# Keys split in halves over partition groups, a product with v over 64 rows in four tiles, and four raw pieces of w_out in flight

## The chip, the cores and the metric

One core of a Trainium2 chip. The metric is the time of one execution on the device in microseconds (us), as the median of several executions. The trace of one execution of each kernel was read as well; its span is about 2 us below the time of the same execution.

A ratio is the mean time of one kernel's runs over that of the kernel before in the same rounds, with a 95% interval. It is not quite the ratio of the medians quoted beside it.

## The reference, cut to what matters

```python
scores = scale * np.matmul(q, k.transpose(0, 1, 3, 2))          # (8, 8, 576, 576)
thresh = np.max(scores, axis=-1, keepdims=True) - tau
scores = np.where(scores >= thresh, scores, -1000000000.0)
attn = np.exp(scores - np.max(scores, axis=-1, keepdims=True))
attn = attn / (np.sum(attn, axis=-1, keepdims=True) + 1e-09)
out  = np.matmul(attn, v)                                       # head_dim 64
# x = out as (4608 tokens, 512)
g = x @ w_gate;  silu = g * (1.0 / (1.0 + np.exp(-g)))          # 512 -> 1536
y = (silu * (x @ w_val)) @ w_out                                # 1536 -> 512
```

Each softmax row needs one maximum and one sum over all 576 keys. That is what the change cuts in two.

## The kernel before: the parts that matter

The kernel walks over segments (a pair of heads of one batch element) and in each over tiles of 128 queries, five to a full segment. The last has 64 queries. While VectorE and ScalarE do the softmax of a tile, TensorE gets a portion of the feed-forward network (gate, value and output products, called fill here). The scores of a tile take both buffers of the PSUM pool `ps_s`. The product with v of the *previous* segment comes during the first tile of a segment and takes its outputs from the same pool.

```python
ps_s = ctx.enter_context(tc.tile_pool(name="ps_s", bufs=2, space=bass.MemoryType.PSUM))
...
def scores(seg, t):
    pss = [ps_s.tile([P, 2, 512], F32, name="sc") for _ in range(2)]       # both buffers
    ... # 4 matmuls: 128 queries x 288 keys, for two heads
    for h in range(m):
        nc.vector.tensor_reduce(out=nmx[:, h:h + 1], in_=scs[h], axis=AX.XY, op=ALU.max, negate=True)
    for h in range(m):
        nc.scalar.activation(ps[h], scs[h], AF.Exp, bias=nmx[:, h:h + 1])
    nc.scalar.activation(th[:, 0:m], nmx[:, 0:m], AF.Identity, bias=cut, scale=-1.0)
    yield
    turn()                                            # transposes of the tile before
    for h in range(m):                                # masking and sum: frees the score buffers
        nc.vector.scalar_tensor_tensor(out=ps[h], in0=scs[h], scalar=th[:, h:h + 1], in1=ps[h],
                                       op0=ALU.is_ge, op1=ALU.mult, accum_out=sm[:, h:h + 1])
    ... # + 1e-9, reciprocal; yield; scaling on ScalarE
...
for n, seg in enumerate(segs):
    for x, t in enumerate(seg["tiles"]):
        go = scores(seg, t); next(go)                 # scores, maxima, exponentials
        ...
        next(go); ...; fill(part); next(go)           # masking, a portion of fill, scaling
        if attends and not alone:                     # first tile of a segment
            next(products); next(products)            # product with v, copies out
        ...
        fill(part)                                    # the other portion
```

## Time and profile before

| | kernel before |
|---|---|
| time | 1779.55 us (1779.41 to 1782.08, 3 runs) |
| first 30 tiles (attention alone, then weights arriving) | 329.3 us |
| the long stage: the other 130 tiles, from their first scores to the last | 1225.8 us |
| from there to the end | 211.5 us |
| TensorE in the long stage: idle, at half clock | 50.8 us, 0 us |

The stages are cut at the start of a tile's scores in the trace, so that the same work lies in each stage of every kernel; the 9 to 10 us before the first scores are left out. The views are in the prediction below.

### The profile page before, as it was taken

What the parts mean: (1) busy time and instruction counts of PE and PEld (TensorE: products, weight loads), DVE (VectorE), ACT (ScalarE), POOL (GpSimd) and SP (SyncE); (2) the same over time, 40 slices, a digit from 0 to 9 for tenths busy, and PEclk for the clock granted to TensorE, in tenths of its full rate; (3) what the DMA queues carried; (4) which work ended last, traced back from release to release, by engine and by line L of the source; (5) the groups of instructions that cost most, each with busy time, mean ns of one, the idle gap of its engine ahead of it and who ended that gap; (6) DMA issues with size and microseconds to landing.
All of it is one profiled execution on the core that took longest, in us unless ns stands there. A gap on an engine that the chain in (4) does not pass through costs nothing.

```text
span 1776.2 us, 35271 instructions
## 1 busy us (share of the span) xinstructions
PE 1587.2 (89%) x15008; PEld 917.8 (52%) x15008; DVE 897.4 (51%) x1978; ACT 708.4 (40%) x1274; POOL 302.1 (17%) x246
## 2 busy tenths in 40 slices
PE   4577862799999999999999999999999999999998
PEld 3444430366855545545555555545545555555554
DVE  7876675465555545555545444544554544521000
ACT  4554542245443535434434443534434434411111
POOL 3233334201110201111010110211011101101111
PEclk9678885799999999999999999999999999999999
DMA  6545122222212121221122122121122112100000
GB/s 165 134 119 140 40 73 71 67 59 48 41 41 53 38 61 35 48 53 20 41 47 51 30 47 53 41 59 31 25 46 54 36 40 52 28 19 1 6 12 18
DMA packets 179179, 90.75 MB, mean 51 GB/s; under 512 B 157520, under 2 KB 163664, under 8 KB 179024
## 3 DMA queue, kind: packets, MB, share of 16 engines
q1 hardware_dynamic: 176144, 79.07, 19.6%
q0 software_dynamic: 2880, 9.44, 1.4%
q8 instruction: 118, 1.93, 0.5%
q14 instruction: 37, 0.30, 0.1%
HBM read 79.04 MB, written 9.44 MB: 50 GB/s over the span
## 4 chain that ended last, share of the span: by engine, by line
PE 75%; issue 5%; DVE 2%; DMA 1%; ACT 1%; POOL 1%; SPq 0%; POOLq 0%; DVEq 0%; ACTq 0%
PE po L356 19%; PE pg L323 19%; PE pv L331 19%; PE xo L273 9%; PE sc L206 7%; PE sc L213 2%; DMA ht<-in_moe_w_out_dram 1%; DVE tmp L149 0%; DVE p L228 0%; POOL tmp L155 0%; DVE tmp L151 0%; POOL ht L342 0%; ACT gt L341 0%; DVE nmx L221 0%; DVE p L244 0%
## 5 line engine op out<-in xcount | busy, mean ns | idle before, releaser
L356 PE MATMUL po<-wo,ht 128*128 128x512 f32 x864 | 397.4, 611 | 52.9 <-POOL wo L158 52.0
L323 PE MATMUL pg<-xT,wg 128*128 128x384 f32 (+1 forms) x1248 | 411.1, 473 | 11.2 <-POOL wg L158 9.1
L331 PE MATMUL pv<-xT,wv 128*128 128x384 f32 (+1 forms) x1248 | 409.3, 472 | 0.4 <-ACT xT L301 0.4
L221 DVE TENSOR_REDUCE nmx<-sc 128x1 f32<-128x576 f32 x288 | 205.6, 750 | 312.9 <-PE sc L206 289.0
L223 ACT ACTIVATE p<-sc,nmx 128x576 f32<-128x576 f32 x288 | 203.4, 741 | 304.8 <-DVE nmx L221 304.2
L323 PEld LDWEIGHTS pg<-xT,wg 128*128 128x128 f32 x1248 | 231.0, 193 | 162.5 <-issue 23.6
L331 PEld LDWEIGHTS pv<-xT,wv 128*128 128x128 f32 x1248 | 230.3, 192 | 152.1 <-issue 25.6
L234 ACT ACTIVATE p<-p,ri 128x576 f32<-128x576 f32 x288 | 209.2, 768 | 218.4 <-DVE ri L231 218.3
L356 PEld LDWEIGHTS po<-wo,ht 128*128 128x128 f32 x864 | 162.3, 193 | 258.3 <-issue 198.1
L228 DVE SCALAR_TENSOR_TENSOR p<-sc,th,p 128x576 f32<-128x576 f32 x288 | 220.5, 797 | 32.3 <-ACT th L224 32.3
L332 DVE TENSOR_TENSOR ht<-gt,pv 128x384 f32<-128x384 f32 (+1 forms) x156 | 80.2, 517 | 283.3 <-PE pv L331 258.8
L273 PE MATMUL xo<-p,vr 32*64 32x128 f32 (+2 forms) x8352 | 170.3, 292 | 53.1 <-issue 42.9
L244 DVE STREAM_TRANSPOSE p<-p 128x576 f32<-128x576 f32 x288 | 207.1, 753 | 0.9 <-ACT p L234 0.9
L342 POOL TENSOR_TENSOR ht<-ht,gt 128x768 f32<-128x768 f32 (+1 forms) x78 | 130.0, 1695 | 444.1 <-ACT gt L341 384.2
L273 PEld LDWEIGHTS xo<-p,vr 32*64 32x64 f32 x8352 | 146.7, 131 | 87.6 <-issue 67.1
L324 ACT COPY gt<-pg 128x384 f32<-128x384 f32 (+1 forms) x156 | 70.1, 449 | 240.3 <-PE pg L323 240.3
L206 PE MATMUL sc<-kT,qT 64*128 64x288 f32 x896 | 143.1, 433 | 5.1 <-DVE p L228 5.1
L186 POOL TENSOR_SCALAR qraw<-qraw,scl 128x576 f32<-128x576 f32 x32 | 55.6, 1737 | 437.1 <-DMA qraw<-in_q_dram 366.3
L206 PEld LDWEIGHTS sc<-kT,qT 64*128 64x128 f32 x896 | 79.0, 188 | 85.7 <-issue 71.2
L293 DVE COPY xT<-xo 128x128 f32<-128x128 f32 (+2 forms) x57 | 13.9, 285 | 175.7 <-PE xo L273 175.7
L361 POOL DMA_DIRECT2D out_dram<-ob x36 | 20.7, 574 | 420.4 <-ACT ob L360 420.4
L360 ACT COPY ob<-po 128x512 f32<-128x512 f32 x36 | 21.0, 584 | 119.0 <-PE po L356 79.7
(51 smaller groups left out, 747.3 us busy)
## 6 DMA issues: line engine op xcount, KB each, us to landing
vr<-in_v_dram SPq DMA_DIRECT2D x280, 144.0 KB, 3.4
qraw<-in_q_dram SPq DMA_DIRECT2D x128, 72.0 KB, 2.3
kraw<-in_k_dram SPq DMA_DIRECT2D x128, 72.0 KB, 2.7
out_dram<-ob POOLq DMA_DIRECT2D x36, 256.0 KB, 2.3
wo<-in_moe_w_gate_dram SPq DMA_DIRECT2D x16, 384.0 KB, 4.3
wo<-in_moe_w_val_dram SPq DMA_DIRECT2D x16, 384.0 KB, 4.4
ht<-in_moe_w_out_dram SPq DMA_DIRECT2D x16, 384.0 KB, 3.0
tau_s<-in_tau_dram SPq DMA_DIRECT2D x1, 0.5 KB
```

The lines of the kernel that those rows point to most:

```text
L206: nc.tensor.matmul(pss[h][:, n, 0:SH], qT[hs, q0:q0 + P], kT[hs, n * SH:(n + 1) * SH], start=True, stop=True)
L221: nc.vector.tensor_reduce(out=nmx[:, h:h + 1], in_=scs[h], axis=AX.XY, op=ALU.max, negate=True)
L223: nc.scalar.activation(ps[h], scs[h], AF.Exp, bias=nmx[:, h:h + 1])
L228: nc.vector.scalar_tensor_tensor(out=ps[h], in0=scs[h], scalar=th[:, h:h + 1], in1=ps[h], op0=ALU.is_ge, op1=ALU.mult, accum_out=sm[:, h:h ...
L234: nc.scalar.activation(ps[h], ps[h], AF.Copy, scale=ri[:, h:h + 1])
L244: nc.vector.transpose(out=p, in_=p)
L273: nc.tensor.matmul(xa[a][h * D:(h + 1) * D, at:at + n * G].rearrange("d (t r) -> d t r", r=G), vr[rs, h, j, :], p[rs, lo:hi, js], start=(j ...
L323: nc.tensor.matmul(ps[:, 0:n], wg[:, c, f * P:(f + 1) * P], x[:, c, cs], start=(c == 0), stop=(c == NCC - 1))
L331: nc.tensor.matmul(ps[:, 0:n], wv[:, c, f * P:(f + 1) * P], x[:, c, cs], start=(c == 0), stop=(c == NCC - 1))
L332: nc.vector.tensor_tensor(out=hts[f // 2][:, f % 2, cs], in0=gts[f // 2][:, f % 2, cs], in1=ps[:, 0:n], op=ALU.mult)
L342: nc.gpsimd.tensor_tensor(out=ht, in0=ht, in1=gt, op=ALU.mult)
L356: nc.tensor.matmul(po, hts[f // 2][:, f % 2, i * P:(i + 1) * P], wo[:, f, :], start=(f == 0), stop=(f == NF - 1))
```

## The change

Its intent: a product with v that contracts over 64 keys in place of 32. That is 72 records on four 64*64 tiles (18 rounds) in place of 288 on eight 32*64 tiles (36 rounds, 7.10 us in the mean of the late products). For this, two groups of 32 partitions must hold two different halves of the keys for the *same* queries. The scores are laid out so from the start: partition group (a, c) holds query group a and key half c. The price is that a row's maximum and sum lie in two groups and must be exchanged (`across`). Besides, v is loaded into two buffers, and w_out arrives in four raw buffers instead of two, with two conversions to a tile.

The diff, cut to its core:

```diff
-                            land2[len(wpieces) % 2]))
+                            land2[len(wpieces) % 4]))
 ...
+    def across(x, n):
+        y = stp.tile([P, 4], F32, name="other")
+        for g in range(NG):
+            nc.vector.tensor_copy(y[g * G:(g + 1) * G, 0:n], x[(g ^ 1) * G:((g ^ 1) + 1) * G, 0:n])
+        return y[:, 0:n]
 ...  # scores: 16 matmuls of 32 output partitions and 288 columns in place of 4 of 128
-        for h in range(m):
-            nc.vector.tensor_reduce(out=nmx[:, h:h + 1], in_=scs[h], axis=AX.XY, op=ALU.max, negate=True)
-        for h in range(m):
-            nc.scalar.activation(ps[h], scs[h], AF.Exp, bias=nmx[:, h:h + 1])
+        for x, tile_ in enumerate(pss):
+            nc.vector.tensor_reduce(out=nmx[:, 2 * x:2 * x + 2], in_=tile_[:, :, 0:SH], axis=AX.X, op=ALU.max,
+                                    negate=True)
+        nc.vector.tensor_tensor(out=nmx[:, 0:m], in0=nmx[:, 0:m], in1=across(nmx, m), op=ALU.min)
+        for x in range(m):                                   # m is 4 now, 2 before
+            nc.scalar.activation(ps[x], scs[x], AF.Exp, bias=nmx[:, x:x + 1])
 ...
-        nc.vector.tensor_scalar(out=sm[:, 0:m], in0=sm[:, 0:m], scalar1=1e-9, scalar2=None, op0=ALU.add)
+        nc.vector.scalar_tensor_tensor(out=sm[:, 0:m], in0=sm[:, 0:m], scalar=1e-9, in1=across(sm, m),
+                                       op0=ALU.add, op1=ALU.add)
 ...  # product with v
-            xo = [ps_s.tile([P, 2, 512], F32, name="xo", tag="sc") for _ in range(2)]
-        for j in range(NJ):
-            for a in range(NG):
-                rs = slice(a * G, (a + 1) * G)
+            xo = ps_s.tile([P, 2, 512], F32, name="xo", tag="sc")
+        for j in range(NK):                                  # NK = NJ // 2
+            for a in range(2):
+                rs = slice(a * D, (a + 1) * D)
 ...  # pacing of the conversions
-            if alone and n >= NP:
+            if n >= NP:
                 weights(1)
```

More of the change, by code (lines that the diff above doesn't have):

```diff
@@ L54 @@
     NJ = S // G
+    NK = NJ // 2
     SM = 512
@@ L113 @@
     land2 = [hp.tile([P, 2, TC], F32, name="ht").rearrange("p n w -> p (n w)") for _ in range(2)]
+    spare = xp.tile([P, NCC, TC // (2 * G), 2, G], F32, name="xT").rearrange("p c t a r -> p (c t a r)")
+    land2 += [spare[:, n * 2 * TC:(n + 1) * 2 * TC] for n in range(2)]
     for f in range(0, NF, nf):
@@ L123, in fetch_weights @@
         for _ in range(n):
-            if not wpieces or len(fetched) + len(split) >= (NL if len(wpieces[0][0].shape) == 2 else 2):
+            if not wpieces or len(fetched) + len(split) >= (NL if len(wpieces[0][0].shape) == 2 else 4):
                 return
@@ L190, in load_v @@
         b, hp_ = divmod(i, NP)
-        vr = ld.tile([P, 2, NJ, D], F32, name="vr")
-        for a in range(NG):
-            for h in range(2):
-                nc.sync.dma_start(out=vr[a * G:(a + 1) * G, h],
-                                  in_=v[b, 2 * hp_ + h].rearrange("(r j) d -> r j d", r=G))
-        return vr
+        vr = ld.tile([P, 2, NK, D], F32, name="vr", bufs=2)
+        for a in range(2):
+            for c in range(2):
+                nc.sync.dma_start(out=vr[(2 * a + c) * G:(2 * a + c + 1) * G].rearrange("r h j d -> r h (j d)"),
+                                  in_=v[b, 2 * hp_:2 * hp_ + 2].rearrange("h (r c j) d -> c r h (j d)", c=2, j=NK)[c])
+        return vr
+    def across(x, n):
[3 more added lines that the diff above has]
+        return y[:, 0:n]
     def scores(seg, t):
@@ L203, in scores @@
             pss = [ps_s.tile([P, 2, 512], F32, name="sc") for _ in range(2)]
-            for n in range(2):
-                for h, hs in enumerate(heads):
-                    nc.tensor.matmul(pss[h][:, n, 0:SH], qT[hs, q0:q0 + P],
-                                     kT[hs, n * SH:(n + 1) * SH], start=True, stop=True)
+            put = [(pss[h], u, h, q0 + u * D) for u in range(2) for h in range(2)]
             at = [tiles.index(t), len(tiles) + tiles.index(t)]
@@ L210, in scores @@
             pss = [ps_s.tile([P, 2, 512], F32, name="sc")]
-            for n, h in ((0, 0), (1, 1), (1, 0), (0, 1)):
-                hs = heads[h]
-                nc.tensor.matmul(pss[0][hs, n, 0:SH], qT[hs, q0:q0 + 2 * G], kT[hs, n * SH:(n + 1) * SH],
-                                 start=True, stop=True)
+            put = [(pss[0], h, h, q0) for h in range(2)]
             at = [tiles.index(t)]
-        m = len(at)
-        nmx, th, sm, ri = (stp.tile([P, 2], F32, name=x) for x in ("nmx", "th", "sm", "ri"))
-        scs = [ps[:, :, 0:SH] for ps in pss]
-        ps = [pt[:, x, :].rearrange("p (n s) -> p n s", n=2) for x in at]
-        for h in range(m):
-            nc.vector.tensor_reduce(out=nmx[:, h:h + 1], in_=scs[h], axis=AX.XY, op=ALU.max, negate=True)
-        for h in range(m):
-            nc.scalar.activation(ps[h], scs[h], AF.Exp, bias=nmx[:, h:h + 1])
+        for x in range(0, len(put), 2):
+            for g in range(NG):
+                a, c = divmod(g, 2)
+                for ps, u, h, col in put[x:x + 2]:
+                    hs = heads[h]
+                    nc.tensor.matmul(ps[g * G:(g + 1) * G, u, 0:SH], qT[hs, col + a * G:col + (a + 1) * G],
+                                     kT[hs, c * SH:(c + 1) * SH], start=True, stop=True)
+        m = 2 * len(at)
+        nmx, th, sm, ri = (stp.tile([P, 4], F32, name=x) for x in ("nmx", "th", "sm", "ri"))
+        scs = [ps[:, u, 0:SH] for ps in pss for u in range(2)]
+        ps = [pt[:, x, u * SH:(u + 1) * SH] for x in at for u in range(2)]
+        for x, tile_ in enumerate(pss):
[4 more added lines that the diff above has]
+            nc.scalar.activation(ps[x], scs[x], AF.Exp, bias=nmx[:, x:x + 1])
         nc.scalar.activation(th[:, 0:m], nmx[:, 0:m], AF.Identity, bias=cut, scale=-1.0)
@@ L226, in scores @@
         turn()
-        for h in range(m):
-            nc.vector.scalar_tensor_tensor(out=ps[h], in0=scs[h], scalar=th[:, h:h + 1], in1=ps[h],
-                                           op0=ALU.is_ge, op1=ALU.mult, accum_out=sm[:, h:h + 1])
-        nc.vector.tensor_scalar(out=sm[:, 0:m], in0=sm[:, 0:m], scalar1=1e-9, scalar2=None, op0=ALU.add)
+        for x in range(m):
+            nc.vector.scalar_tensor_tensor(out=ps[x], in0=scs[x], scalar=th[:, x:x + 1], in1=ps[x],
+                                           op0=ALU.is_ge, op1=ALU.mult, accum_out=sm[:, x:x + 1])
+        nc.vector.scalar_tensor_tensor(out=sm[:, 0:m], in0=sm[:, 0:m], scalar=1e-9, in1=across(sm, m),
+                                       op0=ALU.add, op1=ALU.add)
         nc.vector.reciprocal(out=ri[:, 0:m], in_=sm[:, 0:m])
         yield
-        for h in range(m):
-            nc.scalar.activation(ps[h], ps[h], AF.Copy, scale=ri[:, h:h + 1])
+        for x in range(m):
+            nc.scalar.activation(ps[x], ps[x], AF.Copy, scale=ri[:, x:x + 1])
         for x in at:
@@ L252, in attend @@
         full = [t for t in tiles if t < NT]
-        m = len(full)
+        m = 2 * len(full)
+        p = p.rearrange("p n (u j q) -> p (n u) j q", u=2, q=G)
         if alone:
-            xa = [ps_f.tile([P, 512], F32, name="xa", tag="psf") for _ in range(NG)]
+            xa = [ps_f.tile([P, 512], F32, name="xa", tag="psf") for _ in range(2)]
         else:
-            xo = [ps_s.tile([P, 2, 512], F32, name="xo", tag="sc") for _ in range(2)]
-            xa = [xo[a // 2][:, a % 2, :] for a in range(NG)]
-        for j in range(NJ):
-            js = slice(j * G, (j + 1) * G)
-            for a in range(NG):
-                rs = slice(a * G, (a + 1) * G)
-                for h in range(2):
-                    lo = len(tiles) if h else 0
-                    hi = lo + m
-                    at = P
-                    if tail and h == 0 and a < 2:
-                        hi += 1
-                    if tail and h == 1 and a >= 2:
-                        lo -= 1
-                        at -= G
-                    n = hi - lo
+            xo = ps_s.tile([P, 2, 512], F32, name="xo", tag="sc")
+            xa = [xo[:, a, :] for a in range(2)]
+        for j in range(NK):
+            for a in range(2):
+                rs = slice(a * D, (a + 1) * D)
+                for h in range(2):
+                    lo = h * (m + tail)
+                    at = G - h * tail * G
+                    n = m + tail
                     nc.tensor.matmul(
-                        xa[a][h * D:(h + 1) * D, at:at + n * G].rearrange("d (t r) -> d t r", r=G),
-                        vr[rs, h, j, :], p[rs, lo:hi, js], start=(j == 0), stop=(j == NJ - 1))
+                        xa[a][h * D:(h + 1) * D, at:at + n * G].rearrange("d (i q) -> d i q", q=G),
+                        vr[rs, h, j, :], p[rs, lo:lo + n, j, :], start=(j == 0), stop=(j == NK - 1))
         yield
@@ L280, in attend @@
         per = TC // (2 * G)
-        for w in range(2):
-            put = nc.scalar.copy if w or alone else nc.vector.tensor_copy
-            ts = [first + 2 * t + w for t in full]
-            for j in sorted({x // per for x in ts}):
-                own = [x for x in ts if x // per == j]
-                t0 = ts.index(own[0])
-                dst = xts[j][:, cc, own[0] % per:own[-1] % per + 1:2].rearrange("d t a r -> d a t r")
-                cs = slice(P + t0 * G, P + (t0 + len(own)) * G)
-                if alone:
-                    for a in range(2):
-                        put(dst[:, a], xa[2 * w + a][:, cs].rearrange("d (t r) -> d t r", r=G))
-                else:
-                    put(dst, xo[w][:, :, cs].rearrange("d a (t r) -> d a t r", r=G))
+        puts = deque([nc.scalar.copy] if alone else [nc.vector.tensor_copy, nc.scalar.copy])
+        blocks = [first + 2 * t + u for t in full for u in range(2)]
+        for j in sorted({x // per for x in blocks}):
+            own = [x for x in blocks if x // per == j]
+            i0 = 1 + blocks.index(own[0])
+            dst = xts[j][:, cc, own[0] % per:own[-1] % per + 1]
+            cs = slice(i0 * G, (i0 + len(own)) * G)
+            if alone:
+                for a in range(2):
+                    puts[0](dst[:, :, a, :], xa[a][:, cs].rearrange("d (i q) -> d i q", q=G))
+            else:
+                puts[0](dst.rearrange("d i a q -> d a i q"), xo[:, :, cs].rearrange("d a (i q) -> d a i q", q=G))
+            puts.rotate(1)
         if tail:
@@ L297, in attend @@
                 hs = slice(h * D, (h + 1) * D)
-                c0 = P + m * G if h == 0 else P - G
+                cs = slice((1 + m) * G, (2 + m) * G) if h == 0 else slice(0, G)
                 if alone:
                     for a in range(2):
-                        nc.scalar.copy(xts[j][hs, cc, at, a], xa[2 * h + a][hs, c0:c0 + G])
+                        puts[0](xts[j][hs, cc, at, a], xa[a][hs, cs])
                 else:
-                    (nc.scalar.copy if h else nc.vector.tensor_copy)(xts[j][hs, cc, at], xo[h][hs, :, c0:c0 + G])
+                    puts[0](xts[j][hs, cc, at], xo[hs, :, cs])
+                puts.rotate(1)
         yield
@@ L530 @@
             if not alone:
-                if wpieces or fetched or split:
-                    weights(1)
+                weights(1)
             elif n >= NP or n * len(early) + x < 2 * NCC:
```

## The prediction

> **What bounds the kernel now.** I read the page first (busy shares, slices), then the waits of TensorE by stage, then single stretches of the timeline.
>
> ```profile
> PE 1587.2 (89%) x15008; PEld 917.8 (52%) x15008; DVE 897.4 (51%) x1978; ACT 708.4 (40%) x1274; POOL 302.1 (17%) x246
> PE   4577862799999999999999999999999999999998
> DVE  7876675465555545555545444544554544521000
> ```
>
> Each digit is a slice of 44.4 us. There are three stages: attention alone to 177 us, in which VectorE (DVE) is fuller than TensorE (PE); a stretch to 333 us with a hole in PE; then PE at nine tenths or more. The same by stage (columns PE, PEld, DVE, ACT, POOL, clock, DMA):
>
> ```profile
> 177.00:258.00 81.00, 64.91 (x744) 38.12 (x744) 53.83 (x118) 36.95 (x68) 27.09 (x24) 0.85 0.23 54
> 258.00:333.00 75.00, 23.00 (x40) 8.40 (x40) 43.45 (x76) 22.50 (x40) 33.80 (x31) 0.59 0.26 75
> 333.00:1570.00 1237.00, 1186.24 (x11132) 687.62 (x11128) 650.20 (x1452) 534.03 (x928) 157.03 (x114) 1.00 0.19 44
> ```
>
> The middle row is PE waiting for pieces of w_out. PE's waits before 330 us, and the chain of waits there:
>
> ```profile
> PE po L356 <- POOL wo L158: 52.0, 4, 19.0
> PE sc L206 <- DVE p L228: 35.0, 10, 4.5
> ...
> 296.68 3.06 DMA ht<-in_moe_w_out_dram
> 304.04 3.02 DMA ht<-in_moe_w_out_dram
> 311.35 3.05 DMA ht<-in_moe_w_out_dram
> ```
>
> A load of 3 us stands in the chain every 7.35 us, and each such turn makes two pieces: two raw buffers, so 3.67 us a piece. After 333 us PE is the bound, and what can be won there is PE time. One product with v there, on the PE timeline:
>
> ```profile
> 560.94 0.49 PE L273 MATMUL xo<-p,vr 32*64 32x160 f32 x8 [0.59 <-PE pg L323]
> 561.68 4.04 PE L273 MATMUL xo<-p,vr 32*64 32x128 f32 x220 [0.24 <-issue]
> 566.61 1.33 PE L273 MATMUL xo<-p,vr 32*64 32x160 f32 x60 [0.89 <-issue]
> 567.87 2.85 PE L331 MATMUL pv<-xT,wv 128*128 128x384 f32 x8
> ```
>
> From 560.94 to 567.87 is 6.93 us for 288 records. In the single records each of the eight 32*64 tiles starts a 160-column record every 136 ns, so 36 rounds should take 4.9 us. The rest is a halt after eight records (they await the second head's masking on VectorE) and the 0.89 us halt at "issue". Such halts stand 128 records apart within a product. All 29 late products average 7.10 us.
>
> The softmax of one 128-query tile, whose scores started at 1390.15 (VectorE, then ScalarE):
>
> ```profile
> 1391.42 1.42 DVE L221 TENSOR_REDUCE nmx<-sc 128x1 f32<-128x576 f32 x2 [0.54 <-PE sc L206]
> 1392.76 1.43 DVE L244 STREAM_TRANSPOSE p<-p 128x576 f32<-128x576 f32 x2
> 1394.11 0.77 DVE L228 SCALAR_TENSOR_TENSOR p<-sc,th,p 128x576 f32<-128x576 f32 x1
> 1394.82 0.81 DVE L228 SCALAR_TENSOR_TENSOR p<-sc,th,p 128x576 f32<-128x576 f32 x1
> ...
> 1392.21 1.41 ACT L223 ACTIVATE p<-sc,nmx 128x576 f32<-128x576 f32 x2 [4.08 <-DVE nmx L221]
> 1393.51 0.29 ACT L224 ACTIVATE th<-nmx,cut 128x2 f32<-128x2 f32 x1
> ```
>
> The masking (L228) frees both score buffers 5.5 us after the scores began. The next scores need both, and begin after 6.53 us where two feed-forward pieces lie between, 9.1 us where three do. So only 1.0 us of slack hides this chain.
>
> [...] eight tiles run side by side, and a score group of four rounds at 243 ns (0.97 us) takes 1.17 us from its start to the next group's. [...] an L149 takes 0.36 us alone, 1.04 us beside a GpSimd instruction.
>
> **The change, part by part.**
>
> (1) Product with v. 144 matmuls become 36, so 288 records become 72, of 288 columns on four 64*64 tiles: 18 rounds. A 288-column record follows its predecessor on a tile after 243 ns (L206, L213), so 4.4 us, [...] about 4.65. It uses one PSUM buffer, not two, so the halt for the second head goes[...]. 7.10 - 4.65 = 2.45 us a product.
>
> (2) Scores. 4 matmuls per tile become 16, 32 records on eight 64*32 tiles, again four rounds: 1.17 us, say 1.2.
>
> (3) Softmax. Keys lie in halves over partition groups, so maximum and sum are exchanged between groups. Independent tiny VectorE instructions start 0.07 us apart (L86 to L87), dependent ones 0.18 to 0.20 (L87 to L88, L230 to L231). Four copies and a minimum: 0.04 + 0.21 + 0.15 + 0.04 + 0.17 = 0.6 us. The exponential waits for both heads instead of one: its start moves from 2.06 to 3.33 us after the scores. Four instructions of 288 for two of 576 cost ScalarE 0.14 us (pitch 0.36 against 0.66) and the masking 0.21 us (0.40 against 0.70). Masking starts at 5.1 instead of 3.96 us, frees the first buffer at 6.0, the second at 6.85. The chain is 1.35 us longer, and VectorE has 0.6 + 0.2 + 0.4 = 1.2 us more work a tile.
>
> (4) w_out. Four raw buffers and two conversions a tile in the tiles after 177 us. By the order of the program, eight conversions instead of eleven are left for the burst that PE waits on, and 40 instead of 36 are made before its first output.
>
> Sum by stage. 0 to 177 us: VectorE is nearly full in the first twelve tiles, and 12 x 1.35 = +16 us. In the next eight, products with v took 7 to 10 us (halts and a slow clock) and may take 2.5 to 4: about -12 net of a longer VectorE part, and four tiles pay +1 each: +8 in all. 177 to 333 us: the burst runs at VectorE's and GpSimd's own pace, 3.05 us a piece (two GpSimd L155 at 285.30 and 288.35). 8 x 3.05 plus 6.5 of softmax is 31 us, with its output 33, against 55 for that tile; the tile before it falls from 23 to about 12; the two products with v give 5; against that, five tiles with two conversions each become bound by VectorE at about 10.5 us: net +5. Together -33. 333 to 1570 us: 26 products. Most start 4.6 us after the scores; the longer chain makes that 6.05. So a product gains 2.45 less 1.45 in about 23 cases, the whole in three: -30. Of the 78 other full tiles about 40 have two pieces between and lose 0.35 us, a few delayed by sigmoids more: +19. Scores +4. Net -7. After 1570: the last product, -3. Sum: +8 - 33 - 7 - 3 = -35 us, 1745 us.
>
> **The rivals.** (A) Softmax becomes the bound of the long stage. If the chain grows by 1.8 instead of 1.35 us, 40 tiles lose 0.45 more and 23 products 0.45 more: +28 us, 1773. For it: only 1.0 us of slack, and VectorE at 5.1 us busy in a 6.53 us tile. Against: instruction pitches are read from this trace. (B) Softmax stays hidden and the product pays in full: chain +1.0 or less. Then 26 x 2.4 + 33 gives about 1690. Against it: the wait of a product for the masking is already there (0.59 us idle at 560.94). (C) Eight 64*32 tiles don't run at full rate, four streams to each row half; the trace shows only two. At half rate each score group gains about 1 us, 144 tiles: +130, near 1875. I give it one in twenty. (D) The w_out wait is replaced wholly by VectorE[...]: the gain of 33 shrinks to about 15: 1763.
>
> **Range and chances.** The early stages carry the gain; the long stage is two terms of 20 to 30 us of opposite sign, each uncertain by a half. That gives some 25 us either way: 1712 to 1782. Two per cent is 1744 us, right at my number: faster 0.47, same 0.46, slower 0.07.
>
> **What would show it.** Products with v of 72 records in 4.4 to 4.8 us without halts at "issue"; score groups of 1.2 us; masking freeing buffers near 6.0 and 6.85 us after the scores; new waits of the scores and the product for L241 (masking) of 0.3 to 1.5 us after 333 us; the wait for w_out at 15 to 25 us instead of 52; VectorE near 1,130 us busy. It is wrong if score groups take over 1.4 us, if the first 177 us grow by over 20 us, or if those new waits are absent.

The 4.65 us of the product are 18 rounds of 243 ns (4.37 us) and 0.28 us more, the author's estimate; a score group has 0.20 us beyond its four rounds (1.17 against 0.97 us). And that the halts at "issue" would go with the new product was assumed when the 2.45 us were put down. The pitches of 0.36 and 0.40 us are estimates as well: the trace has instructions of 576 (0.66 and 0.70 us), none of 288.

## More of the kernel before

"Half clock" is time in which the trace gives the clock granted to TensorE as 0.5.

One more line of the page belongs beside the changed kernel's: the chain that ended last, as shares of the span by engine.

```profile
PE 75%; issue 5%; DVE 2%; DMA 1%; ACT 1%; POOL 1%; SPq 0%; POOLq 0%; DVEq 0%; ACTq 0%
```

Three quarters of that chain are matmuls, VectorE (DVE) a fiftieth: a kernel bound by TensorE.

## The result, and the profile after

| | before | changed |
|---|---|---|
| time, same rounds | 1780.32 us (1779.41 to 1782.08) | 1887.62 us (1885.82 to 1887.95) |
| ratio | | 1.0599 (1.0581 to 1.0618) |
| first 30 tiles | 329.3 us | 339.7 us |
| long stage | 1225.8 us | 1325.0 us |
| rest | 211.5 us | 211.3 us |

The kernel became 6% slower; 1745 us were predicted, and 1782 us was the top of the range. Nearly all of the loss is in the long stage. The page of the changed kernel (busy shares, the slices of PE, VectorE and the granted clock, and the chain that ended last):

```profile
PE 1590.0 (84%) x10560; PEld 874.3 (46%) x10560; DVE 1198.3 (64%) x3966; ACT 789.8 (42%) x1807; POOL 301.3 (16%) x246
PE   2447675788788899889989899899989999899998
DVE  6989889576677677766666566766665666641000
PEclk9768877898899999989999999999999999999999
...
PE 47%; DVE 30%; ACT 12%; issue 9%; POOL 1%; DMA 0%; SPq 0%; DVEq 0%; ACTq 0%; POOLq 0%
```

PE's busy time is the same as before (1590.0 against 1587.2 us) though it has three tenths fewer instructions. VectorE has 301 us more. In the chain, VectorE and ScalarE now make 42% where they made 3%: a large part of the time is now set by the softmax. The longest waits of PE, as totals, times and longest, in us:

```profile
PE sc L225 <- DVE p L241: 152.0, 94, 8.1
PE xo L281 <- issue: 68.7, 22, 5.8
PE po L365 <- POOL wo L161: 25.9, 3, 15.9
```

Scores wait 152 us for the masking (38 us before), but only 41 us of that lie in the long stage (3 before); the rest falls to the first 30 tiles. The product with v waits 69 us, put down to "issue" though it is the buffer it waits for, as a stretch shows below. The wait for w_out fell from 52 to 26 us. The long stage in one row (us; busy us of PE, PEld, VectorE, ScalarE, GpSimd with their instructions; granted clock; share and GB/s of the DMA):

```profile
349.10:1674.10 1325.00, 1194.33 (x8191) 669.01 (x8190) 883.83 (x3044) 596.60 (x1360) 153.74 (x111) 0.96 0.13 28
```

PE is idle for 131 us of it in place of 51, and its busy time did not fall, since the clock did: 0.96, where the row of before has 1.00. Two stretches show how. First a tile of 128 queries among others like it, VectorE and then ScalarE. PE began most of its scores at 727.55 and those of the next tile at 735.20:

```profile
728.90 1.42 DVE L232 TENSOR_REDUCE nmx<-sc 128x2 f32<-128x576 f32 x2
730.35 0.68 DVE L205 COPY other<-nmx 32x4 f32<-32x4 f32 x4
731.07 0.16 DVE L234 TENSOR_TENSOR nmx<-nmx,other 128x4 f32<-128x4 f32 x1
731.15 1.43 DVE L258 STREAM_TRANSPOSE p<-p 128x576 f32<-128x576 f32 x2
733.22 0.52 DVE L241 SCALAR_TENSOR_TENSOR p<-sc,th,p 128x288 f32<-128x288 f32 x1 [0.64 <-ACT th L237]
...
735.09 0.68 DVE L205 COPY other<-sm 32x4 f32<-32x4 f32 x4
...
736.56 1.41 DVE L232 TENSOR_REDUCE nmx<-sc 128x2 f32<-128x576 f32 x2
```

```profile
731.33 1.67 ACT L236 ACTIVATE p<-sc,nmx 128x288 f32<-128x288 f32 x4 [0.95 <-DVE nmx L234]
732.87 0.31 ACT L237 ACTIVATE th<-nmx,cut 128x4 f32<-128x4 f32 x1
```

ScalarE can begin its exponentials only when both reductions, four copies and the minimum are done. In the stretch of the prediction it began 0.79 us after the first reduction had begun, here 2.43. Everything behind shifts with it, to the masking, and at its end the next scores start at once. Where tiles follow each other with two pieces of fill between, the kernel before had a period of 6.53 us, set by PE. Here it is 7.65 us, set by this loop: scores, maxima, exchange, exponentials, masking, scores. VectorE has one wait in the period, of 0.64 us, so it is nearly full, too.

In a tile that nothing delays, all times from the start of its scores, the changed kernel starts the exponentials at 3.72 us (before 2.06), the masking at 5.62 (3.96 in the stretch of the prediction), and frees the buffers at 6.57 and 7.45 us (the second at 5.5 before).

The second stretch is a product with v, in a tile that began most of its scores at 797.94:

```profile
804.35 0.52 DVE L241 SCALAR_TENSOR_TENSOR p<-sc,th,p 128x288 f32<-128x288 f32 x1 [1.30 <-ACT th L237]
...
805.52 7.29 PE L281 MATMUL xo<-p,vr 64*64 64x288 f32 x72 [3.61 <-ACT gt L333]
```

It needs one of the two buffers, so it starts when two maskings are done, after 3.61 us of idle PE (the named releaser had long been done). Then it takes 7.29 us for 72 records instead of the 4.71 us of those at full clock. The granted clock falls to 0.5 at 804.09 and comes back at 810.92. In those 6.83 us a round of four records takes 479 ns in place of 240.

The granted clock in this trace is 0.5 or 1.0 and nothing between. In the long stage the lower state stood for 105.8 us (before: 0), in 24 stretches of one to three times 3.41 us. How much idle time came before a fall? In the stretch above PE had been idle for only 2.18 us when the clock fell, and busy for 36% of the 3.41 us before the fall. The whole long stage, its time at full clock cut into steps of 3.41 us, says the same: in 23 of the 24 steps that ended in a fall PE was busy for 0 to 40% and in one for 50%; in the 332 after which the clock stayed up, for 42% or more. So some 2 us of idle time were enough there, while one product ran at full clock after a wait of 3.80 us: the length of a wait did not alone tell whether the clock fell. What decides it was not tested.

By the place of the tile in its segment (26 segments), the long stage's 99 us divide so: the tile with the product +50, the next +7, the third and fourth +28 and +26, the half tile -11. For the 26 products themselves: idle time ahead 12.9 us before and 82.6 after; from the start of the first record to the start of the last 180.0 and 146.5.

### The profile page after: what moved, and what is told of

Its sections match the earlier page's. It is cut to its first block, busy times and chain, and to the rows that moved or that the text cites. A ratio compares the mean times of both kernels' runs of the same rounds, so it can differ in the third digit from the quotient of the medians.

```text
span 1885.3 us, 28929 instructions
## 1 busy us (share of the span) xinstructions
PE 1590.0 (84%) x10560; PEld 874.3 (46%) x10560; DVE 1198.3 (64%) x3966; ACT 789.8 (42%) x1807; POOL 301.3 (16%) x246
## 4 chain that ended last, share of the span: by engine, by line
PE 47%; DVE 30%; ACT 12%; issue 9%; POOL 1%; DMA 0%; SPq 0%; DVEq 0%; ACTq 0%; POOLq 0%
PE po L365 13%; PE pg L332 10%; PE pv L340 9%; PE xo L281 8%; ACT p L236 7%; DVE p L241 7%; DVE nmx L232 7%; DVE other L205 7%; PE sc L225 6%; DVE p L258 2%; ACT p L248 2%; DVE tmp L154 1%; DVE tmp L152 1%; DVE nmx L234 1%; ACT L236 1%
## 5 line engine op out<-in xcount | busy, mean ns | idle before, releaser
L248 ACT ACTIVATE p<-p,ri 128x288 f32<-128x288 f32 x576 | 262.6, 524 | 411.8 <-DVE ri L245 411.8
L365 PE MATMUL po<-wo,ht 128*128 128x512 f32 x864 | 400.4, 615 | 30.5 <-POOL wo L161 25.9
L236 ACT ACTIVATE p<-sc,nmx 128x288 f32<-128x288 f32 x576 | 242.7, 501 | 317.7 <-DVE nmx L234 307.1
L241 DVE SCALAR_TENSOR_TENSOR p<-sc,th,p 128x288 f32<-128x288 f32 x576 | 263.5, 512 | 138.4 <-ACT th L237 138.4
L232 DVE TENSOR_REDUCE nmx<-sc 128x2 f32<-128x576 f32 x288 | 204.9, 748 | 134.2 <-PE sc L225 134.1
L281 PE MATMUL xo<-p,vr 64*64 64x288 f32 (+1 forms) x2088 | 171.2, 485 | 93.8 <-issue 68.7
L225 PE MATMUL sc<-kT,qT 64*32 64x288 f32 x4032 | 186.7, 425 | 65.1 <-DVE p L241 64.3
L281 PEld LDWEIGHTS xo<-p,vr 64*64 64x64 f32 x2088 | 148.3, 164 | 121.9 <-issue 85.4
L341 DVE TENSOR_TENSOR ht<-gt,pv 128x384 f32<-128x384 f32 (+1 forms) x156 | 78.7, 512 | 191.8 <-PE pv L340 170.7
L225 PEld LDWEIGHTS sc<-kT,qT 64*32 64x32 f32 x4032 | 70.7, 109 | 189.2 <-issue 152.7
L205 DVE COPY other<-sm 32x4 f32<-32x4 f32 (+1 forms) x640 | 119.8, 187 | 12.1
L205 DVE COPY other<-nmx 32x4 f32<-32x4 f32 (+1 forms) x640 | 119.8, 187 | 12.0
```

Source lines behind the costliest of these rows:

```text
L205: nc.vector.tensor_copy(y[g * G:(g + 1) * G, 0:n], x[(g ^ 1) * G:((g ^ 1) + 1) * G, 0:n])
L225: nc.tensor.matmul(ps[g * G:(g + 1) * G, u, 0:SH], qT[hs, col + a * G:col + (a + 1) * G], kT[hs, c * SH:(c + 1) * SH], start=True, stop=True)
L232: nc.vector.tensor_reduce(out=nmx[:, 2 * x:2 * x + 2], in_=tile_[:, :, 0:SH], axis=AX.X, op=ALU.max, negate=True)
L236: nc.scalar.activation(ps[x], scs[x], AF.Exp, bias=nmx[:, x:x + 1])
L241: nc.vector.scalar_tensor_tensor(out=ps[x], in0=scs[x], scalar=th[:, x:x + 1], in1=ps[x], op0=ALU.is_ge, op1=ALU.mult, accum_out=sm[:, x:x ...
L248: nc.scalar.activation(ps[x], ps[x], AF.Copy, scale=ri[:, x:x + 1])
```

## The experiments

Sixteen kernels ran. All but e1, e2, e7 and e16 give the right result. This table has them by stage, in us; "product" is the idle time ahead of the 26 products of the long stage in all, and their length in all, from the traces.

| run | time | ratio | first 30 tiles | long stage | PE idle there | half clock there | product: wait, length |
|---|---|---|---|---|---|---|---|
| before | 1780.3 | 1 | 329.3 | 1225.8 | 50.8 | 0 | 12.9, 180.0 |
| changed | 1887.6 | 1.060 | 339.7 | 1325.0 | 130.7 | 105.8 | 82.6, 146.5 |
| e1 no exchange of maxima | 1708.2 | 0.958 | 306.2 | 1180.7 | 44.3 | 13.7 | 31.3, 113.3 |
| e2 new product, old softmax | 1658.7 | 0.930 | 274.8 | 1162.9 | 18.3 | 3.4 | 13.7, 111.6 |
| e3 fill first | 1826.4 | 1.025 | 335.9 | 1268.9 | 89.0 | 44.4 | 9.7, 111.2 |
| e4 before + w_out part | 1753.3 | 0.984 | 302.5 | 1229.5 | 51.7 | 6.8 | 12.9, 180.2 |
| e5 idle matmuls | 1862.6 | 1.045 | 339.3 | 1299.5 | 66.5 | 34.1 | 20.4, 114.4 |
| e6 exchange on ScalarE | 1932.7 | 1.084 | 338.2 | 1372.3 | 165.1 | 133.1 | 82.0, 142.0 |
| e7 no exchange of sums | 1865.4 | 1.047 | 323.6 | 1319.1 | 123.9 | 102.4 | 78.7, 143.5 |
| e8 without w_out part | 1927.1 | 1.081 | 374.8 | 1331.1 | 131.1 | 119.5 | 83.7, 155.0 |
| e9 own maxima | 1850.4 | 1.039 | 345.7 | 1287.3 | 103.9 | 85.3 | 69.3, 140.1 |
| e10 e9, fill first | 1814.3 | 1.020 | 344.2 | 1244.9 | 73.7 | 34.1 | 5.6, 110.0 |
| e11 before + delay | 1909.1 | 1.073 | 366.3 | 1318.2 | 102.3 | 75.1 | 63.1, 194.5 |
| e12 e9, transposes later | 1850.4 | 1.040 | 352.0 | 1273.9 | 101.5 | 78.5 | 70.3, 134.8 |
| e13 e12, fill first | 1810.2 | 1.017 | 350.0 | 1241.0 | 73.8 | 47.8 | 8.1, 110.0 |
| e14 e13, no copies | 1772.9 | 0.997 | 338.7 | 1214.5 | 56.0 | 30.7 | 2.1, 109.7 |
| e15 e4, fill first | 1734.6 | 0.975 | 295.7 | 1209.5 | 42.9 | 0 | about 0, 160.6 |
| e16 copies in one group | 1821.5 | 1.027 | 322.2 | 1275.6 | 101.9 | 64.8 | 73.3, 134.0 |

My theory after reading the traces (T1) was: the exchange lengthens the way from a tile's scores to its freed buffers, and that wait, with the clock that falls in it, is the loss. The rivals: the new product or the layout of the scores is at fault; or VectorE's added amount of work is, wherever it stands.

### The parts of the change: e1, e2, e4, e8

e1 leaves the exchange of the maxima out (wrong: each half uses its own maximum for everything):

```diff
-        nc.vector.tensor_tensor(out=nmx[:, 0:m], in0=nmx[:, 0:m], in1=across(nmx, m), op=ALU.min)
```

> The changed kernel without the exchange of the maximum (wrong result on purpose). Theory 1 (the longer softmax chain holds TensorE up, and the idle before the product with v then halves its clock): the exponential starts about 1.0 us earlier, masking ends near 6.45 us after the scores instead of 7.45, full tiles with two pieces come back towards 6.6 us, the idle before the product falls from 3.2 us to about 2 and the clock stays up: 1760 to 1800 us. Theory 2 (the smaller, more numerous matmuls cost TensorE time of their own): the chain was hidden anyway, 1860 us or more.

It became 1708.17 us, 179 us faster than the changed kernel, more than T1 expected. The stretch of VectorE and then ScalarE in one tile shows that more went than the copies:

```profile
601.66 1.42 DVE L232 TENSOR_REDUCE nmx<-sc 128x2 f32<-128x576 f32 x2 [0.84 <-PE sc L225]
603.00 1.43 DVE L257 STREAM_TRANSPOSE p<-p 128x576 f32<-128x576 f32 x2
604.92 0.52 DVE L240 SCALAR_TENSOR_TENSOR p<-sc,th,p 128x288 f32<-128x288 f32 x1 [0.49 <-ACT th L236]
```

```profile
603.04 1.67 ACT L235 ACTIVATE p<-sc,nmx 128x288 f32<-128x288 f32 x4
604.58 0.31 ACT L236 ACTIVATE th<-nmx,cut 128x4 f32<-128x4 f32 x1
```

In a tile that nothing delays the exponentials start at 2.08 us, 1.64 earlier than in the changed kernel: 1.0 for copies and minimum, and 0.6 because the first head's exponentials run beside the second head's reduction again. (In this stretch ScalarE began at 603.04 only because it had been busy.)

e2 is the changed kernel with the score function of the kernel before, so the new product with the old softmax (wrong, as the layout no longer fits the product):

```diff
     def scores(seg, t):
-        ...  # of the changed kernel
+        ...  # of the kernel before, word for word
```

> The changed kernel with the scores and softmax of the kernel before (wrong result on purpose): only the product with v in four tiles, v in two buffers and the w_out part are new. Theory 1: the product costs 4.65 us instead of 7.1, the clock stays at full speed, and the w_out part gives some 30 us: 1680 to 1715 us. Theory 2 (the product in four tiles is slow of itself, 6.3 us as the median in the changed kernel): 1730 us or more.

1658.67 us. The product's own worth is thus large: the long stage falls by 63 us against before, the products in it by 68 (180.0 to 111.6). With the old softmax neither the shape of the product nor its single buffer costs anything. The difference to e1, 49.5 us, is the rest of the new softmax: four exponentials and maskings in place of two, the exchange of sums, and the scores of 16 matmuls.

e4 is the kernel before with the w_out part alone, e8 the changed kernel without it:

```diff
-                            land2[len(wpieces) % 2]))
+                            land2[len(wpieces) % 4]))
 ...  # limit of pieces in flight 2 -> 4; a second conversion to each tile after the first 20
```

> The kernel before with the w_out part alone: four raw buffers and two conversions a tile after the first stage (right result). As predicted for this part: 1745 to 1760 us, the wait of the output matmuls for pieces of w_out falling from 52 to 15 to 25 us. Rival: VectorE and GpSimd, which make the pieces, only spread the same wait over earlier tiles: 1772 to 1784 us.

> The changed kernel with the weights' part taken back (two raw buffers of w_out, conversion pacing as before); output right. Theory T1: the parts add up; the kernel before gained 27 to 29 us from this part alone, all of it in the stage where w_out is first needed, so the changed kernel loses 20 to 35 us without it: 1908 to 1925 us. Rival T2 (in the changed kernel the longer long stage or the slower start hides the transfer already): within 10 us of 1888.

e4 came to 1753.30 us, 29 us faster than before, and e8 to 1927.09 us, 39 us slower than the changed kernel (35 of them in the first 30 tiles; 20 to 35 had been expected). In e4 the wait for w_out is halved, as in the changed kernel:

```profile
PE po L358 <- POOL wo L160: 24.5, 3, 13.8
```

So two of the three parts are good, and the exchange costs more than both give.

### Where the exchange takes effect: e3, e5, e6, e7, e11

e3 puts the second portion of fill ahead of the product in the first tile of a segment, so that PE has other work while the buffer isn't free:

```diff
             if attends and not alone:
+                fill(part)
                 next(products)
                 next(products)
 ...
-            fill(part)
+            if not attends or alone:
+                fill(part)
```

> The changed kernel with both stretches of feed-forward work ahead of the product with v instead of one before and one behind it (right result). Theory 1: the idle before the product falls from 3.2 us to under 0.7, the clock never halves in the long stage and each product takes 4.65 us; against that the next scores wait about 1.4 us for the product's copies out of PSUM: 1810 to 1845 us. Theory 2 (the idle is only moved, the chain of VectorE sets the pace of the segment): within 1 per cent of 1888 us, the wait turning up at the next scores.

1826.35 us, as T1 expected: the wait ahead of the products fell from 83 to 10 us, and they ran at full clock (111.2 us). Of the 108 us saved there the long stage kept 56. Of the rest 30 us turned up as a new wait: the next tile's scores now follow the product with no fill between, and need the buffer that ScalarE is still copying out. The page of waits of e3's long stage has, besides the wait for the masking as before:

```profile
PE sc L225 <- ACT xT L311: 30.0, 26, 3.2
```

e5 keeps the wait and fills it with three useless matmuls (2.74 us of work each time), to tell the wait from the clock:

```diff
+        if not alone and b:
+            idle = ps_f.tile([P, 512], F32, name="idle", tag="psf")
+            for _ in range(3):
+                nc.tensor.matmul(idle, wg[:, 0, 0:P], wg[:, 0, 0:512], start=True, stop=True)
```

> The changed kernel with three idle matmuls of 512 columns (into a spare PSUM tile, result unused, output right) ahead of each of the 26 products of the long stage, so that TensorE isn't idle while it waits for the buffer. Theory T1: of the loss in the long stage, one part is the wait itself and a second part is the clock[...]: the products take 146 us in place of 111. Keeping the engine busy gives back the clock's part and not the wait: 26 products at some 4.3 us, half-clock time in the long stage from 106 us to 20 to 50 us, total 1840 to 1870 us. Rival T2 (the wait alone is the loss, the clock doesn't matter or falls all the same): within 1% of 1888 us, or slower for the added matmuls[...].

1862.59 us, 25 us faster *with* more work. A stretch of PE:

```profile
793.45 2.74 PE L277 MATMUL idle<-wg 128*128 128x512 f32 x6
797.34 4.71 PE L285 MATMUL xo<-p,vr 64*64 64x288 f32 x72 [1.15 <-ACT gt L337]
```

The product starts no earlier but takes 4.71 us. Half-clock time went from 105.8 to 34.1 us and the products from 146.5 to 114.4. So the clock is a part of the loss by itself.

e6 moves the copies to ScalarE, e7 leaves out the exchange of the sums (wrong):

```diff
-            nc.vector.tensor_copy(y[g * G:(g + 1) * G, 0:n], x[(g ^ 1) * G:((g ^ 1) + 1) * G, 0:n])
+            nc.scalar.copy(y[g * G:(g + 1) * G, 0:n], x[(g ^ 1) * G:((g ^ 1) + 1) * G, 0:n])      # e6
```

```diff
-        nc.vector.scalar_tensor_tensor(out=sm[:, 0:m], in0=sm[:, 0:m], scalar=1e-9, in1=across(sm, m),
-                                       op0=ALU.add, op1=ALU.add)
+        nc.vector.tensor_scalar(out=sm[:, 0:m], in0=sm[:, 0:m], scalar1=1e-9, scalar2=None, op0=ALU.add)   # e7
```

> The changed kernel with the four tiny copies of each exchange (maxima and sums) on ScalarE in place of VectorE; output right. Theory T1: the long stage loses because the chain from a tile's scores to its freed buffers is longer, so whichever engine makes the copies, the chain counts: a copy on ScalarE has its own fixed time (a tiny activation took about 0.18 us here: the threshold), and each exchange crosses engines twice; I expect the chain no shorter and the time within 2% of 1888 us, 1870 to 1925 us. Rival T2 (VectorE's added work of 1.4 us a tile is the bound, not the chain): 1790 to 1840 us, since ScalarE is busy only 44% of the long stage.

> The changed kernel without the exchange of the sums (each half divides by its own sum; wrong result on purpose), the exchange of the maxima kept. Theory T1: the sums' exchange comes after the masking, by which the score buffers are already free; it delays only the scaling and the transposes ahead of the product and takes 0.9 us of VectorE a tile, so it counts far less than the maxima's exchange, whose removal gave 180 us: I expect 1820 to 1870 us. Rival T2 (what counts is VectorE's work, equal for both exchanges): about as much as without the maxima's, 1700 to 1740 us.

e6: 1932.67 us, just past the top of what T1 expected, though VectorE's busy time fell from 1198 to 975 us. The exponentials started at 3.83 us at the earliest, where the changed kernel has 3.72. e7: 1865.43 us, a gain of 22 us where leaving out the exchange of the maxima gave 179. In the long stage the gains are 6 us and 144 us. The two have the same copies on the same engine; they differ in where they stand. With the changed kernel's order, VectorE's amount of work is not what sets the period.

e11 gives the kernel before the delay and little else: four tiny copies of the maxima, each within its own partitions, and a minimum that changes no value.

```diff
+        same = stp.tile([P, 2], F32, name="other")
+        for g in range(NG):
+            nc.vector.tensor_copy(same[g * G:(g + 1) * G, 0:m], nmx[g * G:(g + 1) * G, 0:m])
+        nc.vector.tensor_tensor(out=nmx[:, 0:m], in0=nmx[:, 0:m], in1=same[:, 0:m], op=ALU.min)
```

> The kernel before with four tiny copies of the negated maxima (each to the same partitions) and one minimum of them put between the maxima and the exponentials; output right and unchanged. Nothing else of the change. Theory T1 (the delay of the exponentials behind both maxima and the copies is the cause, whatever the product with v): the chain to the freed buffers becomes 1.5 to 1.7 us longer as in the changed kernel, and the time rises by 100 to 180 us, to 1880 to 1960 us. Rival T4 (the delay hurts only together with the new product, its single buffer or its shape): within 2% of 1781 us.

1909.06 us, 130 us slower with the right result: 37 us in the first 30 tiles and 92 in the long stage. Its trace has the exponentials at 3.70 us, the masking at 5.29 and the buffers free at 6.10 and 6.84. The products wait 63 us in place of 13, and 75 us at half clock appear. The five operations are work for VectorE as well, but in the long stage it is busy for only 770 of the 1318 us, so there it is the delay that costs, whatever the product. In the first 30 tiles the two are not told apart.

### Taking the exchange out of the way: e9, e10, e12, e13, e14

If only the delay of the exponentials counted, a kernel that does the exchange *beside* them should be nearly as fast as e1. e9 does that with a right result: each half takes the exponential against its own maximum, and its sum and reciprocal are corrected later by exp(own minus common maximum).

```diff
-        nc.vector.tensor_tensor(out=nmx[:, 0:m], in0=nmx[:, 0:m], in1=across(nmx, m), op=ALU.min)
+        nc.vector.tensor_tensor(out=gm[:, 0:m], in0=nmx[:, 0:m], in1=across(nmx, m), op=ALU.min)
+        nc.vector.tensor_tensor(out=fa[:, 0:m], in0=gm[:, 0:m], in1=nmx[:, 0:m], op=ALU.subtract)
         ...  # exponentials with nmx; threshold from gm
+        nc.scalar.activation(fa[:, 0:m], fa[:, 0:m], AF.Exp)
 ...
+        nc.vector.tensor_tensor(out=sm[:, 0:m], in0=sm[:, 0:m], in1=fa[:, 0:m], op=ALU.mult)   # before across(sm)
 ...
+        nc.vector.tensor_tensor(out=ri[:, 0:m], in0=ri[:, 0:m], in1=fa[:, 0:m], op=ALU.mult)   # after the reciprocal
```

> The changed kernel with the exchange of the maxima kept, but taken out of the way of the exponentials: each half's exponentials use that half's own maximum; the common maximum is found meanwhile on VectorE for the threshold, and each half's sum and reciprocal are corrected by exp(own minus common maximum). Output right. VectorE has three tiny operations a tile more than the changed kernel (some 0.5 us), ScalarE one. Theory T1 (what counts is how long after its scores a tile frees its two score buffers; VectorE's amount of work doesn't): exponentials start 2.1 us after the scores as without the exchange, buffers freed as there, total 1705 to 1745 us. Rival T2 (VectorE's added work is what costs): no gain or slower, 1880 to 1930 us.

> The same as the run before it, with both portions of the gate, value and output products put ahead of the product with v in the long stage (as in the run with the fill first). Output right. Theory T1: fill first gives TensorE other work while the product waits for its buffer, so what idle ahead of products is left (31 us without the exchange) and the half clock go: another 10 to 30 us, 1685 to 1725 us. Rival T3 (with the chain short the wait is hidden already, and the fill moved is missing behind the product): within 0.5% of the run before, or slower.

e9: 1850.36 us, a clear miss. The exponentials start at 2.08 us as wanted, but the masking at 5.1 in place of 4.0: VectorE does the exchange, then the transposes, then the masking, and the transposes, which had been hidden beside the exponentials, no longer are. e10 gains another 36 us, as e3 did, and misses its range with e9. So T1 as I had put it, with the chain alone, fell. e12 moves the transposes behind the masking, e13 puts the fill first as well:

```diff
-        turn()
+        if t == tiles[0]:
+            turn()
         ...  # masking, sums, reciprocal
+        turn()
         yield
```

> As the run with each half's own maximum (1850 us), but VectorE transposes the tile before after this tile's masking in place of before it, except in the first tile of a segment, ahead of whose product they are needed. Output right. Theory T1 (the loss is how long VectorE's queue keeps the masking back, in whatever way): masking starts 4.0 us after the scores as without the exchange in most tiles, and the time falls by 50 to 110 us, to 1740 to 1800 us. Rival T2 (VectorE's amount of work, which is the same here): within 1% of 1850 us.

> As the run before it, with both portions of the fill ahead of the product in the long stage. Output right. T1: fill first was worth 36 us there with 104 us idle in the long stage; here less is left, so another 15 to 40 us: 1710 to 1775 us. T2: 1814 us within 1%, as the same without the moved transposes.

e12: 1850.44 us, no change; e13: 1810.19 us. Both are what the rival T2 said. The masking starts at 4.0 us now in tiles that nothing delays, but where tiles follow each other VectorE is full (its stretch over one period, PE's scores not waited for):

```profile
819.17 1.43 DVE L264 STREAM_TRANSPOSE p<-p 128x576 f32<-128x576 f32 x2
820.53 1.38 DVE L232 TENSOR_REDUCE nmx<-sc 128x2 f32<-128x576 f32 x2
821.95 0.68 DVE L205 COPY other<-nmx 32x4 f32<-32x4 f32 x4
...
823.19 0.52 DVE L244 SCALAR_TENSOR_TENSOR p<-sc,th,p 128x288 f32<-128x288 f32 x1 [0.17 <-ACT th L238]
...
825.33 0.69 DVE L205 COPY other<-sm 32x4 f32<-32x4 f32 x4
...
826.54 1.43 DVE L264 STREAM_TRANSPOSE p<-p 128x576 f32<-128x576 f32 x2
```

From 819.17 to 826.54 are 7.37 us, with one wait, of 0.17 us. Two limits lie close together: the loop over ScalarE in the changed kernel at 7.65 us, and VectorE's own work at 7.37 us with the three operations of e9 more. Either is above the 6.5 us that PE needs for such a tile.

e14 therefore takes operations away: each exchange is four operations that take one operand from the other group, in place of four copies and one operation.

```diff
-        nc.vector.tensor_tensor(out=gm[:, 0:m], in0=nmx[:, 0:m], in1=across(nmx, m), op=ALU.min)
+        for g in range(NG):
+            a, b = slice(g * G, (g + 1) * G), slice((g ^ 1) * G, ((g ^ 1) + 1) * G)
+            nc.vector.tensor_tensor(out=gm[a, 0:m], in0=nmx[a, 0:m], in1=nmx[b, 0:m], op=ALU.min)
 ...  # the sums in the same way
```

> As the run before it, with each exchange as four operations that take one operand from the other partition group, in place of four copies and one operation, so one tiny operation (0.17 us) less in each exchange. Output right, unless VectorE doesn't take two partition groups as operands of one operation; then it is wrong and only its time counts. T1: the exchange is hidden behind the exponentials there, and one operation less after the masking counts little: 5 to 15 us faster than the run before. T2 (amount of work on VectorE): about 2 x 0.17 x 160 tiles = 54 us off the engine's work, 20 to 50 us faster.

1772.88 us, 37 us faster than e13 for two operations a tile, in the range of T2. Here, with VectorE full, its amount of work does count. This is the fastest version with the new product and a right result, 0.3% below the kernel before.

### The size of one copy: e16

The prediction took 0.07 us between tiny copies; they were 0.175 us apart. The 0.07 us were between two instructions that both cover all 128 partitions (L86 to L87); each of the four copies reads and writes other groups of 32 partitions than the one before. e16 has as many copies of the same shape, within one group (wrong):

```diff
-        for g in range(NG):
-            nc.vector.tensor_copy(y[g * G:(g + 1) * G, 0:n], x[(g ^ 1) * G:((g ^ 1) + 1) * G, 0:n])
-        return y[:, 0:n]
+        for g in range(NG):
+            nc.vector.tensor_copy(y[0:G, 4 * g:4 * g + n], x[0:G, 0:n])
+        return x[:, 0:n]
```

> The changed kernel with the four tiny copies of both exchanges made within partitions 0 to 31 (to four places), and the minimum and the sum taking the tile's own values: as many instructions, same shapes, wrong result on purpose. Theory H (a copy that changes the partition group waits until the one before has ended): they start about 0.07 us apart in place of 0.175, the exponentials start at about 3.3 us after the scores in place of 3.7, VectorE loses 0.8 us of work a tile, and the time falls by 40 to 80 us, to 1808 to 1848 us. Rival (tiny copies of 32 partitions take 0.17 us anywhere): exponentials at 3.7 us and the time within 1% of 1888 us.

1821.46 us, in the range. The stretch of VectorE beside that of the changed kernel, where the four took 0.68 us:

```profile
701.30 0.37 DVE L205 COPY other<-nmx 32x4 f32<-32x4 f32 x4
701.71 0.16 DVE L234 TENSOR_TENSOR nmx<-nmx 128x4 f32<-128x4 f32 x1
```

They start 0.07 us apart. Each copy is about as long (0.15 against 0.16 us), but in one group they overlap, while those that change the group start 0.175 us apart, after the one before has ended. So the copies of these two kernels behave as theory H said.

### A faster kernel: e15

The kernel before with the w_out part and with both portions of fill ahead of the product, and no exchange (the two diffs of e4 and e3):

> The kernel before with the weights' part of the change (1753 us) and both portions of the fill ahead of the product in the long stage; nothing else of the change. Output right. The products there waited 13 us in all and no clock was lost, so T1 expects 5 to 15 us: 1738 to 1750 us. Rival: the fill that then is missing behind the product leaves the next tile's wait open: within 0.5% of 1753 us or slower.

1734.57 us (1727.75 to 1743.96), ratio 0.9753 (0.9715 to 0.9792), result right. A little better than expected: besides the wait ahead of them, the products themselves became shorter (180.2 to 160.6 us). PE's waits of the product at "issue" fell from 49.5 to 26.8 us over the whole kernel. Within the 26 products two kinds of halt shrank: those after the first eight records, 22 in e4 and 5.4 us in all, are gone, and the later ones fell from 28.7 to 22.3 us. Why the later ones fell was not tested. It beats both kernels.

## Why the prediction was wrong, point by point

**The bound (right for before, overtaken after).** In the kernel before PE was the bound after 333 us, and e2 shows that a shorter product pays in full there. The change moved the bound, as rival A of the prediction said; but A was given 1773 us.

**(1) The product (right, with one thing not seen).** 4.65 us were predicted, and it is 4.64 at full clock to the start of the next matmul, without the halts at "issue" that were to go. In 18 of the 26 the half clock falls into it, and it takes 5.9 to 7.6 us. The prediction knew that the product would wait longer and never asked what the clock does when PE waits for 3 us (3.2 us in the mean here, with 71 of the 105.8 us at half clock inside the products). The 26 products took 146.5 us in place of the 111.2 of e3, which ran at full clock: 35 us.

**(2) The scores (right).** 1.13 us a group against 1.17 before, where 1.2 was predicted. Rival C (half rate in eight tiles) is refuted.

**(3) The softmax chain (the step that failed, twice).** First its size. "Independent tiny VectorE instructions start 0.07 us apart" was read from two instructions over the same 128 partitions; the copies, which change the partition group, started 0.175 us apart, and the exchange took 1.0 us instead of 0.6. The four exponentials and maskings were low too (0.38 and 0.44 us apart instead of 0.36 and 0.40), and VectorE got 1.9 us more work a tile (301 us over 160) instead of 1.2. The buffers came free at 6.57 and 7.45 us instead of 6.0 and 6.85, so the chain grew by 1.97 us instead of 1.35. At rival A's rate (63 places that lose what the chain grows) this makes 39 us more, an estimate: 1784 us, still over 100 below the result. e16, with the pitch of the prediction, frees them at 6.26 and 7.13 and takes 66 us less.

Second, what such a delay costs. e11 has nearly the chain of the prediction, free at 6.10 and 6.84, with the old product. Its long stage grew by 92 us. In the prediction, chain and tiles came to 52 us (products 26 times 2.45 less the 30 they were to gain, so 33; tiles 19). The products' wait rose by 50 us in e11, and they became 14 us longer, with 75 us at half clock; the prediction had 33 for the one and nothing for the other. So even with the right pitch the sum would have missed: in e16 the changed kernel is still 2.7% slower than before.

**(4) w_out (right, the wait a little above its range).** It was to fall to 15 to 25 us; it is 25.9. e4 gives 29 us for this part alone (27 of them in the first 30 tiles), e8 39 us in the changed kernel, against 33 predicted. In the changed kernel the gain of the first 30 tiles was eaten: they grew by 10.4 us, where a loss of 8 and a gain of 33 were to make -25. By the table the exchange of the maxima costs them 33.5 us (339.7 against 306.2), the rest of the new softmax 31 (306.2 against 274.8).

**The sum.** +8 - 33 - 7 - 3 was predicted; the spans give +21 (first 20 tiles), -11 (next 10), +99 and 0, together +109. The difference of 144 us is for nearly three quarters the long stage. What of it stays open: how the 57 us by which the long stage of e16 misses its predicted -7 divide between the half clock (64.8 us of it, so some 27 us of busy time lost, an estimate: half of the 54.9 us of matmuls run in it, as a round took 479 ns there in place of 240 in the changed kernel) and the tiles where waits pile up; and whether another order of VectorE's queue could bring e9 further. No run tells these apart. Two figures of the prediction don't follow from its own terms: 1.2 us a tile on 897 us make 1,089 us of VectorE and not 1,130 (it was 1198), and 25 us either way of 1745 is narrower than 1712 to 1782. Of its three signs of being wrong, one came true: the first stage grew by over 20 us (21 in the first 20 tiles). The new waits for the masking stood, but were longer than 0.3 to 1.5 us ahead of the product: 3.2 us in the mean.

## What to carry to other kernels

Before a layout splits a reduction over partitions, count the exchange on the way that hands buffers back, not in instructions: here 1.6 us behind the maxima cost 179 us, and the same copies behind the masking 22 us. Where PE waits for a buffer, look at the granted clock of the work after it: here the products waited 3.2 us in the mean, 18 of the 26 ran partly at half clock, and the 26 took 146.5 us in place of 111.2. Or give PE other work first; that alone was worth 61 us in the changed kernel and some 15 to 19 us on top of the w_out part (by ratios and by times). And undo a mixed change part by part: two of its three parts were gains, and one of them with a change of order is 2.5% faster than the kernel before.
